# Batch 0 of a packed-attention SwiGLU kernel: one written order, with unsplit fp32 output products

## The chip, the cores and the metric

The kernel runs on one core of a Trainium2 chip. The metric is the device time of one launch in microseconds (us), and lower is better. The times below are medians of several runs; the profile is one execution, recorded by the hardware profiler.

## What is computed

Eight batches of eight heads, 576 positions and 64 features per head go through two attentions. In the first, 32 packed queries `p` attend to `k` and `v`; in the second, `q` attends to the 32 packed rows. The result, 4608 tokens by 512 features, goes through a gated feed-forward layer of width 1536.

```
def sm_attn(qq, kk, vv):
    s = scale * np.matmul(qq, kk.transpose(0, 1, 3, 2))
    s = s - np.max(s, axis=-1, keepdims=True)
    a = np.exp(s)
    a = a / (np.sum(a, axis=-1, keepdims=True) + 1e-09)
    return np.matmul(a, vv)
p_packed = sm_attn(p, k, v)
out = sm_attn(q, p_packed, p_packed)
...
g = x @ w_gate
silu = g * (1.0 / (1.0 + np.exp(-g)))
val = x @ w_val
return (silu * val @ w_out).astype(np.float32)
```

The three weight matrices arrive as 64-bit floats and are converted on the chip.

## The kernel before, in words

**Tiling.** Each batch is 576 tokens. The width 1536 is cut into 12 columns `fc` of 128 (gate and value side by side), and each `fc` is worked in two half chunks: A with 256 tokens and B with 320. Below, "2A" is half chunk A of `fc` 2, and a *quad* is the four half chunks of two neighbouring columns (2A, 2B, 3A, 3B). A half chunk is two sets of six matrix products (L439): the first set gives the gate, the second the value.

**The folded product.** The attention output is never formed. `m_part` multiplies the packed rows (`ppt`) with the gate and value weights `w`, and `gv_chunk` multiplies the result with the attention weights `a2`. Each factor is split into a high part (`mh`, `a2h`) and a low part (`ml`, `a2l`) of a reduced-precision type, and three products of parts stand for one exact one. ScalarE (ACT) makes the high part, VectorE (DVE) the low one. Then ACT computes `sg` (Silu, L446) from the gate set and DVE multiplies it with the value set into `hf` (L451; for B also 64 leftover tokens, L454).

**Output products.** `out_mm` (L459) multiplies `h`, split into `hh` and `hl`, with `w_out`, split into `wo_h` and `wo_l`: three products of 512 columns for each 128 tokens, gathered over the 12 columns in four accumulators `acc`.

**Batch 0** is special, because the weights have to be loaded (`load_w`, `load_wout`) and converted (`convert_w`, `convert_wout`: two passes on ACT, L106 and L107, then three on DVE, L108 to L110). A first loop over the 12 columns computes all half chunks and keeps `h` in `kept`; conversions run two columns ahead. A second loop then does all output products. Batch 1's attention (`aux_of`) is interleaved in both loops. From batch 1 on, output products follow the gate and value products one column behind.

**Buffers.** `gv` has two accumulators, one per set; the gate accumulator is free when Silu has read it, the value accumulator when `hf` (and L454) has. `aux` has two, `sg` one. Loads of weights, `k` and `q` share four `io` buffers, and all are issued by one queue (SyncE, SP), in order.

**Order.** TensorE's (PE) instructions stand in the order in which the program writes them. Those of the other engines are placed by a scheduler, except that from batch 1 on some are pinned to the written order (`pin`).

Of the kernel before, what the change touches and what calls it, by code (L numbers as in the profile page):

```python
# [12 lines left out]
I32 = mybir.dt.int32  # L13
# [13 lines left out]
SC, NSC = 96, 6  # L27
# [14 lines left out]
def tile_pack_attention_swiglu(ctx: ExitStack, tc: tile.TileContext, qT, kT, v, vq, pT, wgv, wout, out):  # L42
# [19 lines left out]

    wide = [True]
# [10 lines left out]
    def ps():  # L74
        turn[0] += 1
        if wide[0] and turn[0] % 2:
            return ps_acc.tile([P, 512], F32, tag="acc", name="acc_aux")
        if wide[0] and turn[0] % 4:
            return ps_gv.tile([P, 512], F32, tag="gv", name="gv_aux")
        return ps_aux.tile([P, 512], F32, tag="aux", name="aux")  # L80
# [19 lines left out]
    def f64_convert(dst, st, shape):  # L100
# [5 lines left out]
        nc.scalar.activation(dst, hi.bitcast(F32), AF.Abs)  # L106
        nc.scalar.activation(lo.bitcast(F32), lo.bitcast(U32), AF.Identity, bias=minus_two, scale=LOW_WORD)  # L107
        nc.vector.tensor_scalar(dst, dst, F64_HI_LEAST, F64_HI_MOST, op0=ALU.max, op1=ALU.min)  # L108
        nc.vector.scalar_tensor_tensor(d, d, 3, lo, op0=ALU.logical_shift_left, op1=ALU.bitwise_or)  # L109
        nc.vector.scalar_tensor_tensor(d, hi, 0x3FFFFFFF, d, op0=ALU.bitwise_or, op1=ALU.bitwise_and)  # L110

    sts, sto, wos = {}, {}, {}
# [4 lines left out]
    def convert_w(fc):  # L117
        f64_convert(w_t[fc // 2][:, :, fc % 2, :], sts.pop(fc), NHP)

    def load_wout(fc):  # L120
        sto[fc] = io_tile([P, 1024, 2], I32, "st")
        nc.sync.dma_start(
            sto[fc].rearrange("p (f n) two -> p f (n two)", f=2), wout[fc : fc + 2].rearrange("f p n -> p f n")
        )

    def convert_wout(fc):
        f = wos[fc] = pool.tile([P, 2, DM], F32, tag="wf", bufs=1, name="wo_f")
        f64_convert(f, sto.pop(fc), 2)

    def slot(dtype, name):  # L130
        return pool.tile([P, DM], dtype, tag="slot", bufs=2 * NFC + 2, name=name)

    wo_h, wo_l = {}, {}
# [9 lines left out]
    def load_k(b):  # L143
        p_t = pool.tile([P, NHP, NP], F32, tag="p", bufs=2, name="p_t")
        (nc.sync if b else nc.scalar).dma_start(p_t, pT[b])
        k_t = io_tile([P, 2, NHP, HS], F32, "k_t")
        for hf in range(2):
# [3 lines left out]
    def load_v(b):  # L151
        if b < NEARLY:
            vs[b] = pool.tile([SC, NSC, H * D], F32, tag="v", bufs=1, name="v_t")
            nc.sync.dma_start(vs[b], v[b])
# [4 lines left out]
    def load_q(b):  # L159
        qs[b] = io_tile([P, 2, NHP, HS], F32, "q_t")  # L160
# [10 lines left out]
    def s1_scores(b, direct):  # L171
# [21 lines left out]
        if direct:  # L193
# [6 lines left out]
            nc.vector.tensor_tensor(rs[:, 0], rs[:, 1], rs[:, 2], op=ALU.add)  # L200

    def s1_exp(b):
        t1, rs, nm = st1[b]
        for par in range(NPAR):
            nc.scalar.activation(
                t1[:, par], t1[:, par], AF.Exp, bias=nm[:, 1, par : par + 1], scale=SCALE, accum_out=rs[:, 0, par : par + 1]
            )

    def s1_post(b):
        t1, rs, _ = st1.pop(b)  # L210
        nc.vector.tensor_scalar(rs[:, 1], rs[:, 0], 1e-9, None, op0=ALU.add)
        nc.vector.reciprocal(rs[:, 2], rs[:, 1])
        a1 = pool.tile([SC, NPAR * NSC, P], F32, tag="a1", bufs=1, name="a1")
        for i in range(0, NPAR * NSC, 4):
            p_t = ps()
            for x in range(4):
                par, c = divmod(i + x, NSC)
                nc.tensor.transpose(p_t[:SC, x * P : (x + 1) * P], t1[:, par, c * SC : (c + 1) * SC], ident)
            copy(
                nc.vector if wide[0] and i == 4 else nc.scalar,  # L220
                a1[:, i : i + 4], p_t[:SC].rearrange("p (c x) -> p c x", x=P),
# [4 lines left out]
        for par in range(NPAR):  # L226
            for c in range(NSC):
# [467 lines left out]
```

## Time and profile before

| | us |
|---|---|
| median of 3 runs | 795.68 (795.36 to 798.3) |
| the profiled execution's own time | 794.16 |
| its span in the profile | 792.4 |
| first gate product of batch 0 | 28.89 |
| first gate product of batch 1 | 150.52 |

In the profile, PE is TensorE's products and PEld its weight loads; DVE is VectorE, ACT ScalarE, POOL GpSimd and SP the queue that issues transfers. A row of the timeline gives start and duration in us, then engine, line, operation, what is written and read, the shape and the count; in brackets stands the idle time ahead of it and what ended that. A row of the groups gives busy time and the mean duration in ns of one instruction. A product in full fp32 appears as two records, one per pass.

### The profile page before, as it was taken

To read this page: it belongs to the slowest core of one execution; us is meant where nothing else is said; L and a number is where in the kernel's file an instruction comes from. 1 tells how busy PE (TensorE), PEld (TensorE's weight loads), DVE (VectorE), ACT (ScalarE), POOL (GpSimd) and SP (SyncE) were. 2 spreads that over 40 slices of the span, in tenths; PEclk is the share of its full clock that TensorE was granted. 3 is DMA by queue.
4 is the path that set the end of the run, shared out by engine and by line. 5 is a ranking of instruction groups with operands and counts; after the bars stand their busy time and mean duration, and the time that the engine had idled before them with its cause. 6 is when DMAs were issued, how large, how long until landed. Compare 5 with 4: busy or idle time off the path is not lost.

```text
span 792.4 us, 14383 instructions
## 1 busy us (share of the span) xinstructions
PE 741.8 (94%) x5866; PEld 598.2 (76%) x5866; DVE 458.4 (58%) x1022; ACT 381.5 (48%) x702; POOL 18.3 (2%) x25
## 2 busy tenths in 40 slices
PE   4469788999999999999999999999999999999998
PEld 2346566778787787878778787777888787888886
DVE  3998786454575545755475554754566454653434
ACT  3679664454452545464272643655362542643331
POOL 0001122000000000000000000000000000000000
PEclk9699999999999999999999999999999999999999
DMA  9866742220301211020301103010101000010001
GB/s 319 303 225 249 257 164 80 94 65 10 119 1 67 67 66 61 27 92 3 101 27 67 65 3 127 1 55 3 67 2 53 15 3 2 1 53 2 1 1 66
DMA packets 19777, 59.10 MB, mean 75 GB/s; under 512 B 5952, under 2 KB 6976, under 8 KB 17216
## 3 DMA queue, kind: packets, MB, share of 16 engines
q1 hardware_dynamic: 19568, 58.12, 21.0%
q8 instruction: 46, 0.75, 0.4%
q14 instruction: 19, 0.16, 0.1%
q10 hardware_dynamic: 144, 0.07, 0.0%
HBM read 48.69 MB, written 9.49 MB: 73 GB/s over the span
## 4 chain that ended last, share of the span: by engine, by line
PE 74%; ACT 13%; DVE 7%; DMA 3%; issue 3%; SPq 0%; DVEq 0%; ACTq 0%
PE gv L439 32%; PE acc L459 29%; PE aux L169 6%; PE aux L459 4%; ACT L446 4%; PE aux L332 2%; ACT sg L446 2%; DMA st<-in_wout 1%; DVE ml L90 1%; ACT mh L84 1%; DVE w L109 1%; ACT hh L84 1%; DMA st<-in_wgv 1%; ACT L375 1%; ACT L280 1%
## 5 line engine op out<-in xcount | busy, mean ns | idle before, releaser
L439 PE MATMUL gv<-a2h,ml 128*128 128x256 f32 (+1 forms) x768 | 175.3, 310 | 24.6 <-ACT sg L446 10.0
L439 PEld LDWEIGHTS gv<-a2h,ml 128*128 128x128 f32 x768 | 128.8, 191 | 60.5 <-ACT sg L446 16.9
L439 PE MATMUL gv<-a2l,mh 128*128 128x256 f32 (+1 forms) x768 | 166.2, 298 | 1.1 <-DVE a2l L397 1.1
L446 ACT ACTIVATE sg<-gv 128x256 f32<-128x256 f32 x192 | 79.2, 412 | 179.7 <-PE gv L439 138.2
L439 PE MATMUL gv<-a2h,mh 128*128 128x256 f32 (+1 forms) x768 | 165.7, 297 | 0.0
L459 PE MATMUL acc<-wo_h,hl 128*128 128x512 f32 x384 | 156.5, 407 | 5.0 <-DVE hl L90 5.0
L451 DVE TENSOR_TENSOR hf<-gv,sg 128x256 f32<-128x256 f32 x168 | 70.7, 421 | 140.0 <-PE gv L439 122.5
L459 PE MATMUL acc<-wo_l,hh 128*128 128x512 f32 x384 | 151.4, 394 | 0.0
L459 PE MATMUL acc<-wo_h,hh 128*128 128x512 f32 x384 | 150.9, 393 | 0.0
L439 PEld LDWEIGHTS gv<-a2l,mh 128*128 128x128 f32 x768 | 125.0, 191 | 1.7 <-DVE a2l L397 1.7
L439 PEld LDWEIGHTS gv<-a2h,mh 128*128 128x128 f32 x768 | 125.3, 192 | 0.0
L84 ACT CAST hh<-hf 128x256 fp32r<-128x256 f32 x168 | 67.8, 404 | 111.7 <-DVE hf L451 111.7
L90 DVE TENSOR_TENSOR hl<-hf,hh 128x256 fp32r<-128x256 f32 x168 | 71.1, 423 | 81.6 <-ACT hh L84 81.1
L459 PEld LDWEIGHTS acc<-wo_h,hl 128*128 128x128 f32 x384 | 72.5, 189 | 51.4 <-issue 35.7
L459 PEld LDWEIGHTS acc<-wo_h,hh 128*128 128x128 f32 x384 | 72.5, 189 | 16.6
L459 PEld LDWEIGHTS acc<-wo_l,hh 128*128 128x128 f32 x384 | 72.7, 189 | 9.6
L90 DVE TENSOR_TENSOR ml<-aux,mh 128x512 fp32r<-128x512 f32 (+1 forms) x106 | 62.4, 628 | 19.3 <-ACT mh L84 19.3
L169 PE MATMUL aux<-w,ppt 64*32 64x512 f32 (+1 forms) x848 | 56.3, 566 | 5.4 <-ACT t L189 5.3
L84 ACT CAST mh<-aux 128x512 fp32r<-128x512 f32 (+1 forms) x106 | 52.1, 544 | 5.6 <-PE aux L169 2.9
L446 ACT ACT_TABLE_LOAD x33 | 42.3, 1283 | 11.3 <-issue 10.6
L107 ACT ACTIVATE st<-st,minus_two 128x1024 f32<-128x1024 uint32 x18 | 22.3, 1242 | 0.0
L169 PEld LDWEIGHTS aux<-w,ppt 64*32 64x32 f32 x848 | 10.4, 106 | 14.6 <-ACT t L189 6.2
(127 smaller groups left out, 616.9 us busy)
## 6 DMA issues: line engine op xcount, KB each, us to landing
st<-in_wgv SPq DMA_DIRECT2D x12, 1024.0 KB, 6.6
k_t<-in_kT SPq DMA_DIRECT2D x16, 576.0 KB, 4.9
q_t<-in_qT SPq DMA_DIRECT2D x16, 576.0 KB, 4.8
out<-ot SPq DMA_DIRECT2D x36, 256.0 KB, 2.1
v_t<-in_vq SPq DMA_DIRECT2D x6, 1280.0 KB, 5.6
st<-in_wout SPq DMA_DIRECT2D x6, 1024.0 KB, 5.6
v_t<-in_v SPq DMA_DIRECT2D x2, 1152.0 KB, 13.4
p_t<-in_pT SPq DMA_DIRECT2D x7, 64.0 KB, 2.9
```

Of the source, the lines that this page charges most:

```text
L84: e.copy(dst, src)
L90: lo.tensor_tensor(dst_l, src, dst_h.bitcast(F32), op=ALU.subtract)
L107: nc.scalar.activation(lo.bitcast(F32), lo.bitcast(U32), AF.Identity, bias=minus_two, scale=LOW_WORD)
L109: nc.vector.scalar_tensor_tensor(d, d, 3, lo, op0=ALU.logical_shift_left, op1=ALU.bitwise_or)
L169: nc.tensor.matmul(outs[par][32 * hp : 32 * hp + 32], lhs(r, hp), rhs(r, hp), start=True, stop=True)
L280: late.append(lambda hs=hs: pin(nc.scalar.activation(e[:, :, hs, :SQ], e[:, :, hs, :SQ], AF.Exp, scale=SCALE)))
L332: nc.tensor.matmul(p_p[D * par : D * par + D, NP * hp : NP * hp + NP], v_t[:, par, hp, k, :], a1[:, par, hp, k, :], start=(k == 0), stop=( ...
L375: pin(nc.scalar.activation(x, x, AF.Exp, scale=SCALE))
L439: nc.tensor.matmul(pg[:, :n], m_[:, g, f, s * P : (s + 1) * P], a_[:, g, off : off + n], start=(i == 0), stop=(i == 5),)
L446: nc.scalar.activation(sg[:, :n], pgs[0][:, :n], AF.Silu)
L451: nc.vector.tensor_tensor(hf, pgs[1][:, o : o + 256], sg[:, o : o + 256], op=ALU.mult)
L459: nc.tensor.matmul(acc[:, :], h_[:, c : c + P], w_[fc], start=(fc == 0 and i == 0), stop=(fc == NFC - 1 and i == 2),)
```

## The change

Batch 0 becomes one loop. Five half chunks behind each half chunk, its output products follow, as single fp32 products of the unsplit `h` and the unsplit `w_out`; nothing in batch 0 is split for them. DVE and ACT, too, follow the written order in batch 0: each half chunk calls `between` after its Silu, which issues a fixed portion of the conversions (now generators, advanced by `steps`). The high and low parts of `w_out` are made during batch 1 and the last products of batch 0 (`split_wout`), the low part on DVE where GpSimd made it before. Further edits: `v` of batches 0 and 1 lies in five chunks of 128 rows (the last one of 64) where it was six of 96; 24 products of `ident` with itself (`warm_up`) are put into the start; the exponentials of the first attention are issued one parity at a time; `m_part` can leave its low parts for `m_lows`.

```diff
-SC, NSC = 96, 6
+NSC = -(-S // P)
...
     def split_wout(fc):
-        f = wos.pop(fc)
-        for i in range(2):
-            wo_h[fc + i], wo_l[fc + i] = slot(F32R, "wo_h"), slot(F32R, "wo_l")
-            split(wo_h[fc + i], wo_l[fc + i], f[:, i], hi=nc.scalar, lo=nc.gpsimd)
+        k, i = divmod(fc, 2)
+        if i == 0:
+            wo_h[k], wo_l[k] = pair(F32R, "wo_h"), pair(F32R, "wo_l")
+        pin(nc.scalar.copy(wo_h[k][:, i], wos[k][:, i]))
+        pin(nc.vector.tensor_tensor(wo_l[k][:, i], wos[k][:, i], wo_h[k][:, i].bitcast(F32), op=ALU.subtract))
...
         nc.scalar.activation(sg[:, :n], pgs[0][:, :n], AF.Silu)
         if late:
             late.pop(0)()
+        between()
...
+            def outs(i):
+                fc, is_b = divmod(i, 2)
                 for c in range(2):
-                    out_mm(accs[2 * i + c], *h, c * P, fc)
+                    nc.tensor.matmul(
+                        accs[2 * is_b + c], half(i)[:, c * P : c * P + P], wos[fc // 2][:, fc % 2],
+                        start=(fc == 0), stop=(fc == NFC - 1),
+                    )
+                    yield
...
+                a, b_, o = 2 * k + 2, 2 * k + 3, ("out", k - 1)
+                more = a < NFC
+                def between():
+                    if slot == 0:
+                        steps(o, 5)
+                        if more:
+                            steps(a, 2)
+                    elif slot == 1 and more:
+                        steps(a, 2)
+                        steps(b_, 2)
+                    elif slot == 2 and more:
+                        steps(a, 1)
+                        steps(b_, 1)
+                    elif slot == 3:
+                        if more:
+                            steps(b_, 2)
+                        steps(("out", k), 2)
+                gv_chunk(0, fc, bool(is_b), nothing, half(i), between)
...
+                for t, _ in enumerate(outs(i - LAG) if i >= LAG else ()):
+                    if t == 0 and slot == 3 and more:
+                        m_part(0, k + 1, both)
+                next(aux, None)
...
+                    if b == 1 and fc > 1 and count[0] in (3, 7):
+                        split_wout(fc - fc % 2 + count[0] // 7) if fc % 2 == 0 else None
```

PE in the middle of batch 0. In the kernel before, around 5B to 6A, gate and value products follow each other, with only small products of `m_part` or of batch 1's attention between them:

```order
L439 MATMUL gv<-a2h,mh 128x320 x2
L246 MATMUL aux<-ident,pp 128x128
L439 MATMUL gv<-a2h,ml 128x256 x2
L439 MATMUL gv<-a2l,mh 128x256 x2
L439 MATMUL gv<-a2h,mh 128x256 x2
L169 MATMUL aux<-w_86,ppt 32x256 x8
L439 MATMUL gv<-a2h,ml 128x256 x2
```

In the changed kernel, at 5B, the end of the quad of columns 4 and 5:

```order
L465 MATMUL gv<-a2h,mh 128x320 x2
L624 MATMUL acc<-wo_f,h_324 128x512
L179 MATMUL aux<-w_84,ppt 32x512 x8
L624 MATMUL acc<-wo_f,h_324 128x512
L179 MATMUL aux<-q_t,ppt 32x288 x8
L465 MATMUL gv<-a2h,ml 128x256 x2
```

Two fp32 output products now stand after every half chunk, and `m_part` comes once a quad for both columns, between them.

DVE in batch 0, before: the scheduler puts a half chunk's multiplication (`h`, L451) between the passes of a conversion (`w_85`, L108 to L110), and takes passes of two conversions in turn:

```order
L451 TENSOR_TENSOR h_311<-gv,sg 128x256
L109 SCALAR_TENSOR_TENSOR w_85<-w_85,st 128x4x256
L108 TENSOR_SCALAR w_85<-w_85 128x4x256
L451 TENSOR_TENSOR h_311<-gv,sg 128x256
L454 TENSOR_TENSOR t_301<-gv,sg 128x64
L110 SCALAR_TENSOR_TENSOR w_85<-st,w_85 128x4x256
L109 SCALAR_TENSOR_TENSOR w_85<-w_85,st 128x4x256
```

DVE in the changed kernel, at the first two half chunks of columns 4 and 5:

```order
L421 TENSOR_TENSOR ml<-aux,mh 128x512 x2
L113 TENSOR_SCALAR wo_f<-wo_f 128x1024
L114 SCALAR_TENSOR_TENSOR wo_f<-wo_f,st 128x1024
L115 SCALAR_TENSOR_TENSOR wo_f<-st,wo_f 128x1024
L478 TENSOR_TENSOR h_325<-gv,sg 128x256
L113 TENSOR_SCALAR w_84<-w_84 128x4x256
L114 SCALAR_TENSOR_TENSOR w_84<-w_84,st 128x4x256
L478 TENSOR_TENSOR h_325<-gv,sg 128x256
L481 TENSOR_TENSOR t_318<-gv,sg 128x64
```

Each multiplication now stands behind the two or three conversion passes of its own half chunk, and passes that depend on each other stand next to each other.

ACT in batch 1, before, over half chunks without attention work:

```order
L446 ACTIVATE sg<-gv 128x320
L84 CAST hh<-hf 128x256
L446 ACTIVATE sg<-gv 128x256
L84 CAST hh<-hf 128x256
L84 CAST mh<-aux 128x512 x2
```

and in the changed kernel:

```order
L472 ACTIVATE sg<-gv 128x320
L89 CAST hh<-hf 128x256
L472 ACTIVATE sg<-gv 128x256
L89 CAST hh<-hf 128x256
L144 CAST wo_h<-wo_f 128x512
L472 ACTIVATE sg<-gv 128x320
```

The high part of one column of `w_out` now stands ahead of a Silu, ten times in batch 1; the low part follows on DVE. From batch 2 on all engines have the order they had.

More of the change, by code (lines that the diff above doesn't have):

```diff
@@ L399, in tile_pack_attention_swiglu, with m_lows, m_part @@
     ms = {}
-    def m_part(b, k, fcs):
+    lows = []
+    def m_lows():
+        while lows:
+            nc.vector.tensor_tensor(*lows.pop(0), op=ALU.subtract)
+    def m_part(b, k, fcs, low=True):
         if (b, k) not in ms:
@@ L485, in aux_of @@
             yield from s1_scores(d, False)
-            if d + 1 < B:
-                load_k(d + 1)
-            s1_exp(d)
+            for par in range(NPAR):
+                late.append(lambda par=par: s1_exp(d, par))
+            yield
             yield
@@ L498, in aux_of @@
             yield
-        if d + 1 < B:
+        if NEARLY <= d < B - 1:
             load_v(d + 1)
@@ L604, in tile_pack_attention_swiglu @@
                 while late:
                     late.pop(0)()
+                run_all(outs(i))
                 next(aux, None)
-            if fc == NFC - 2:
-                for _ in aux:
-                    while late:
-                        late.pop(0)()
-                m_part(1, 0, both)
+                if i == 2 * NFC - 2:
+                    m_part(1, 0, both)
+                    split_wout(0)
+                    split_wout(1)
+            for _ in aux:
+                pass
+            load_q(2)
```

286 lines of the change are left out of this document (176 added, 110 removed).

## The prediction

> **What bounds the kernel now.** I read the page first, then busy time by stage, then PE's timeline and waits.
>
> ```profile
> span 792.4 us, 14383 instructions
> PE 741.8 (94%) x5866; PEld 598.2 (76%) x5866; DVE 458.4 (58%) x1022; ACT 381.5 (48%) x702; POOL 18.3 (2%) x25
> ```
> ```profile
> 30.00:60.00 30.00, 22.54 (x196) 16.49 (x196) 28.91 (x52) 19.32 (x36) 0.00 (x0) 0.90 0.70 233
> 60.00:90.00 30.00, 26.02 (x262) 19.94 (x266) 24.48 (x43) 25.10 (x43) 5.23 (x4) 0.94 0.63 225
> 109.00:150.00 41.00, 36.00 (x174) 27.84 (x159) 26.84 (x49) 18.57 (x37) 7.45 (x6) 0.96 0.29 106
> 150.00:240.00 90.00, 88.70 (x714) 71.69 (x713) 52.20 (x124) 44.69 (x81) 0.20 (x1) 1.00 0.18 61
> ```
> ```profile
> 28.89 0.80 PE L439 MATMUL gv<-a2h,ml 128*128 128x256 f32 x2 [9.62 <-ACT a2h L396]
> ...
> 60.02 1.40 PE L169 MATMUL aux<-w,ppt 64*32 64x256 f32 x16 [3.48 <-ACT t L189]
> ...
> 97.84 0.90 PE L439 MATMUL gv<-a2h,ml 128*128 128x320 f32 x2 [1.43 <-DVE h L451]
> ...
> 121.44 0.79 PE L459 MATMUL acc<-wo_h,hl 128*128 128x512 f32 x1 [5.00 <-DVE hl L90]
> ...
> 150.52 0.40 PE L439 MATMUL gv<-a2h,ml 128*128 128x256 f32 x2
> ```
>
> The columns of the stages are PE, PEld, DVE, ACT and POOL, then granted clock, DMA share and GB/s. From 150 on PE is busy 88.7 of 90 us at clock 1.00: only PE work counts there. Batch 0 is the other regime. PE's first gate product stands at 28.89, batch 1's at 150.52, and in the 121.6 us between them DVE, ACT and PE take turns: from 30 to 60 DVE is full (28.91 of 30) and PE is not. The change can gain here alone, and can lose here and, through the moved splits, in batch 1.
>
> **The products: PE work.** The next rows are PE's timeline; the pace is the distance of starts.
>
> ```profile
> 18.14 0.40 PE L169 MATMUL aux<-q_t,ppt 64*32 64x288 f32 x1
> ...
> 18.38 0.40 PE L169 MATMUL aux<-q_t,ppt 64*32 64x288 f32 x1
> ...
> 104.48 0.72 PE L169 MATMUL aux<-q_t,ppt 64*32 64x288 f32 x16
> 105.13 0.51 PE L439 MATMUL gv<-a2h,ml 128*128 128x256 f32 x2
> ...
> 106.67 0.53 PE L439 MATMUL gv<-a2h,ml 128*128 128x320 f32 x2
> ...
> 108.69 0.71 PE L169 MATMUL aux<-q_t,ppt 64*32 64x288 f32 x16
> ...
> 127.22 0.39 PE L459 MATMUL acc<-wo_h,hl 128*128 128x512 f32 x1
> ...
> 137.87 0.39 PE L459 MATMUL acc<-wo_h,hh 128*128 128x512 f32 x1
> ...
> 146.63 1.09 PE L169 MATMUL aux<-w,ppt 64*32 64x512 f32 x16
> 147.65 0.50 PE L459 MATMUL acc<-wo_h,hl 128*128 128x512 f32 x1
> ```
>
> From 127.22 to 137.87 lie 47 split products, 0.2266 us each, so three cost 0.68. No full-size fp32 product is in this trace. From below: an fp32 pass over 288 columns took 0.24 (18.14 to 18.38), so 512 columns take 0.427, two passes 0.853. From above: `m_part`'s two passes over 512 took 1.02 with both ends. I take 0.89, near the lower end, because consecutive products stream like the lower row. The 48 products then cost 42.7 us against 32.6 for 144 split ones: +10.1 of PE work (+8.3 to +16.4), not below zero in any case. [...]
>
> Half chunk A takes 1.54 (105.13 to 106.67), B 2.02, so a quad 7.1. A quad has eight output products (7.1) and `m_part` (1.02).
>
> **The conversions and the written order.** These are groups by line, with mean ns of one, and two DVE rows of the timeline.
>
> ```profile
> L106 ACT ACTIVATE w<-st 128x1024 f32<-128x1024 f32 x12 | 13.8, 1154 | 7.3 <-DMA st<-in_wgv 7.3
> L107 ACT ACTIVATE st<-st,minus_two 128x1024 f32<-128x1024 uint32 x18 | 22.3, 1242 | 0.0
> L108 DVE TENSOR_SCALAR w<-w 128x1024 f32<-128x1024 f32 x12 | 9.1, 764 | 4.3 <-ACT w L106 4.2
> L109 DVE SCALAR_TENSOR_TENSOR w<-w,st 128x1024 int32<-128x1024 int32 x12 | 14.6, 1220 | 0.9 <-ACT st L107 0.7
> L110 DVE SCALAR_TENSOR_TENSOR w<-st,w 128x1024 int32<-128x1024 int32 x12 | 14.6, 1214 | 0.1
> ...
> L446 ACT ACT_TABLE_LOAD x33 | 42.3, 1283 | 11.3 <-issue 10.6
> L446 ACT ACTIVATE sg<-gv 128x256 f32<-128x256 f32 x96 | 37.1, 387 | 82.9 <-PE gv L439 42.8 <-DVE ot L86 20.4 <-DVE s L355 12.3
> L205 ACT ACTIVATE t<-t,nm 128x576 f32<-128x576 f32 x2 | 1.6, 778 | 0.0
> L375 ACT ACTIVATE s<-s 128x576 f32<-128x576 f32 x16 | 10.9, 684 | 0.1
> L451 DVE TENSOR_TENSOR hf<-gv,sg 128x256 f32<-128x256 f32 x168 | 70.7, 421 | 140.0 <-PE gv L439 122.5 <-ACT sg L446 17.1
> L90 DVE TENSOR_TENSOR ml<-aux,mh 128x512 fp32r<-128x512 f32 x84 | 54.0, 684 | 19.1 <-ACT mh L84 19.1
> L84 ACT CAST mh<-aux 128x512 fp32r<-128x512 f32 x84 | 45.0, 588 | 4.7 <-PE aux L169 2.0
> L370 DVE TENSOR_REDUCE r<-s 128x18 f32<-128x576 f32 x16 | 11.9, 745 | 0.1
> L394 DVE STREAM_TRANSPOSE t<-s 128x576 f32<-128x576 f32 x16 | 12.4, 773 | 0.2
> L84 ACT CAST wo_h<-wo_f 128x512 fp32r<-128x512 f32 x12 | 7.1, 619 | 7.9 <-DVE wo_f L110 4.8 <-DVE hl L90 3.1
> ```
> ```profile
> 84.59 1.21 DVE L109 SCALAR_TENSOR_TENSOR w<-w,st 128x1024 int32<-128x1024 int32 x1
> 85.83 1.23 DVE L110 SCALAR_TENSOR_TENSOR w<-st,w 128x1024 int32<-128x1024 int32 x1
> ```
>
> A conversion is 2.3 us on ACT (1.15 + 1.24, overlapped by 0.1) and 3.2 on DVE. Passes that depend on each other start 1.24 apart, so the written order, which sets them side by side, pays them in full. `hf` stands behind `between`'s passes on DVE; who waits is PE, whose value set needs the accumulator that `hf` frees, and Silu, whose one `sg` buffer `hf` frees.
>
> *Start.* The exponentials now go ahead of the first weight conversion; I put the first transposes of q scores on DVE at 18.0. From there to `hf` of 0A DVE's row is closed: two halves of six 128x576 steps (0.75 each, small ones 0.5: 10.0), four transposes (0.45 estimated: 1.8), two half-size `ml` (0.8) and a conversion (3.2), 15.8 together: 33.8. Then 0A to 1B are a chain. 0B's gate set and the next `m_part` on a cold PE, `mh`, Silu: 3.7. ACT's conversion 2.3, DVE's step 1.2, `hf` and L454 0.6: 4.1. Silu 0.4, ACT's conversion 2.3, two DVE steps 2.4, `hf` 0.6: 5.7. Maxima 0.8, copies 0.4, `m_part` 1.0, `mh` and `ml` 1.8, scores 0.65: 4.6. Column 2 starts at 51.9.
>
> *Quads k = 1 to 4.* ACT has three conversions (6.9), four Silus (1.7), two `mh` (1.2): 9.8. DVE has 9.6, four `hf` and two L454 (2.1), two `ml` (1.4): 13.1. PE has 15.2 (k = 1: 13.4). Batch 1's attention comes on top. k = 1: two exponentials between Silus, four table loads (5.1), 1.6, and two copies (about 1.0), so ACT 17.5. k = 2: the product with `v` (about 1.3) and scores (0.65 by 104.48), PE 17.2. k = 3: four transposes, two maxima with subtraction, one sum (1.8 + 3.0 + 1.2), DVE 19.1. k = 4: four scalings or transposes, a sum, a low part (3.1 + 1.2 + 0.75), DVE 18.2. Together 72.0. Each quad closes with a hand-over, `m_part`, `mh`, `ml`, before the next gate set, in which the bound engine partly waits. Records of independent DVE steps overlap by some 0.08, which gives a little back. Followed operation by operation, the four take 18.7, 18.3, 18.9 and 19.2: 75.1.
>
> *Tail.* Quad 5 is PE work: 7.1, then output products of nine half chunks overall (18 x 0.89 = 16.0), `m_part` 1.0, and 0.9 of waiting for the last `w_out` conversion: 25.0.
>
> Batch 0 ends at 51.9 + 75.1 + 25.0 = 152.0 where it ended at 150.5: **+1.5**. The two serial loops become one, and most of what that saves goes to the dearer products and to dependences.
>
> *Edits taken at nothing.* The 24 `warm_up` products run while PE waits for `p`, for exponentials and (28.89) up to 9.62 us for `a2h`; uncovered they would cost some 5. `v`'s load moves the same bytes. The order of loads changes on SP's queue: weight loads now stand behind batch 1's `v`, which waits for batch 0's product with `v` near 16.
>
> ```profile
> st<-in_wgv SPq DMA_DIRECT2D x12, 1024.0 KB, 6.6
> ```
>
> A load lands 6.6 after its issue, and the buffers free at least 8 ahead of use; only batch 1's `q`, wanted one half chunk (4 us) after its buffer frees, is near, at most 2 us.
>
> *Batch 1.* Ten columns of `w_out` are split: 0.62 on ACT ahead of a Silu, 0.68 on DVE (by `ml`). PE works 1.4 on output products between `hh` and the next gate set, so they fit; I take 0.7, bounds 0 and 6.2.
>
> *Clock.* I add 0.6 for one cold spell on PE's path. The sum is 1.5 + 0.7 + 0.6 = **+2.8**. Against the profiled execution's own 794.16 (span and 1.76 around it) this makes 797.0; the median of the runs lies 1.5 higher, so 798.5.
>
> **The rivals.**
>
> *Faster: the engines overlap better than I followed.* The quads at their sums less the overlaps (70), the start at 48, the tail at 24 give 142, thus 8.5 less than before: 787. For it: the kernel before idles on PE too (22.54 of 30). Against it: `hf` behind the passes. It decides if PE waits less than 1 us a quad.
>
> *Slower: the clock.* Two short waits suffice to halve PE's pace: `m_part` took 1.40 after 3.48 idle, and 97.84 shows a pair at 0.90 (0.53 warm, 106.67) after 1.43. Each quad ends with two waits of 1 to 2 us. A spell of 3.4 at half pace costs 1.7; five of them 8.5: 804 to 807. It decides if the granted clock falls below 0.9 between 50 and 125, and if PE is within 1.7 of the bound there. [...]
>
> *Slower: the splits in batch 1.* If a Silu is late each time, 10 x 0.62 goes onto PE's path: 803. The waits of PE from 150 to 240 (total, times, longest, in us) stand against it:
>
> ```profile
> PE gv L439 <- ACT sg L446: 0.9, 2, 0.6
> ```
>
> PE waited 0.9 for Silu in that whole stage.
>
> **How the numbers follow.** The forecast has 0.45, by itself 793 to 803 (products at 0.853 or 1.02, `q` late or not, each stage's second digit); the first rival 0.25, the clock 0.18, the splits 0.12. A measurement can tell 0.5%, 4.0 us, from no change. Faster by more: the first rival, 0.25. Within: 0.33 of the forecast, 0.04 of the splits, 0.37. Slower: 0.12 of the forecast, 0.18 and 0.08, 0.38. The range is 787 to 807: about 0.1 lies beyond each end.
>
> **What would show it.** Right: fp32 passes 0.43 to 0.46 apart; column 2's first gate set near 52; quads of 18 to 19, the third and fourth with DVE full; batch 1's first gate set near 152 to 153; batch 1 as long as before within 1. Wrong: quads under 17 or over 21, or PE idle for a load, or a batch 1 over 2 longer.

## The result, and the profile after

The changed kernel takes 796.6 us (median of 20 runs, 795.73 to 800.43); the kernel before, run beside it, takes 796.62 (20 runs, 794.36 to 798.37). The ratio is 1.0007, with a 95% interval of 0.9996 to 1.0019: no difference that a measurement can tell. The forecast was 798.5, within 787 to 807. The profiled execution of the changed kernel took 796.16 us, against 794.16 before: +2.0 where the sum said +2.8.

Two lines of the page of the changed kernel, and its group of the fp32 output products (busy time and mean ns of one record, then the idle time ahead):

```profile
span 794.4 us, 14060 instructions
PE 750.8 (95%) x5750; PEld 590.0 (74%) x5750; DVE 457.5 (58%) x1002; ACT 376.2 (47%) x670; POOL 2.0 (0%) x13
...
L624 PE MATMUL acc<-wo_f,h 128*128 128x512 f32 x96 | 45.9, 598 | 0.9 <-DVE wo_f L115 0.9
```

PE is 9.0 us busier, and the span is only 2.0 longer. The stages of the changed kernel (PE, PEld, DVE, ACT, POOL, granted clock, DMA share, GB/s), first the start, then cut at the first gate set of each quad, of the tail and of batch 1, show where that went:

```profile
30.00:52.00 22.00, 13.59 (x106) 9.48 (x107) 13.83 (x24) 12.67 (x19) 0.00 (x0) 0.77 0.40 143
51.20:69.69 18.49, 14.69 (x91) 9.56 (x85) 12.50 (x21) 17.67 (x24) 0.00 (x0) 1.00 0.68 232
69.69:88.32 18.63, 18.23 (x183) 11.20 (x181) 12.71 (x21) 10.46 (x15) 0.00 (x0) 1.00 0.63 233
88.32:106.61 18.29, 15.63 (x104) 9.51 (x97) 15.72 (x25) 14.44 (x17) 0.00 (x0) 1.00 0.62 226
106.61:125.85 19.24, 15.82 (x81) 9.53 (x81) 17.45 (x29) 11.55 (x15) 0.20 (x1) 1.00 0.46 151
125.85:150.57 24.72, 23.60 (x101) 13.20 (x101) 10.71 (x17) 5.77 (x10) 0.00 (x0) 1.00 0.43 152
```

In the first quad ACT is the fullest engine (17.67 of 18.49), in the second PE (18.23 of 18.63), in the fourth DVE (17.45 of 19.24), in the tail PE (23.60 of 24.72). In the third no engine is full: DVE and PE are level (15.72 and 15.63 of 18.29). The clock is 1.00 from 51.20 on, and 0.77 in the start.

PE's timeline gives the first gate set of each quad, and the waits at two hand-overs:

```profile
51.20 0.50 PE L465 MATMUL gv<-a2h,ml 128*128 128x256 f32 x2
...
69.28 0.66 PE L226 MATMUL aux<-ident,t 128*128 128x128 f32 x4 [2.71 <-DVE ml L421]
69.69 0.57 PE L465 MATMUL gv<-a2h,ml 128*128 128x256 f32 x2
...
88.32 0.50 PE L465 MATMUL gv<-a2h,ml 128*128 128x256 f32 x2
...
106.61 0.38 PE L465 MATMUL gv<-a2h,ml 128*128 128x256 f32 x1 [1.18 <-DVE ml L421]
...
123.31 1.09 PE L179 MATMUL aux<-w,ppt 64*32 64x512 f32 x16 [1.84 <-DVE w L115]
...
125.85 0.38 PE L465 MATMUL gv<-a2h,ml 128*128 128x256 f32 x1 [0.39 <-DVE ml L421]
...
142.68 5.42 PE L624 MATMUL acc<-wo_f,h 128*128 128x512 f32 x12 [0.91 <-DVE wo_f L115]
148.03 1.09 PE L179 MATMUL aux<-w,ppt 64*32 64x512 f32 x16
...
150.57 0.58 PE L465 MATMUL gv<-a2h,ml 128*128 128x256 f32 x1
```

Batch 0 ends at 150.57 where it ended at 150.52. From 142.68 to 148.03 lie 12 fp32 records, 0.446 us each: a product costs 0.89, as taken.

Batch 1 is where the profile lost its 2 us. The next batch's first gate set stands at 248.84 (246.87 before), so batch 1 takes 98.27 instead of 96.35; after it, both kernels take the same. PE's waits from 150 to 249, then ACT's rows and PE's row at one of the two:

```profile
PE gv L465 <- ACT sg L472: 2.7, 2, 1.6
```
```profile
168.10 0.69 ACT L297 ACTIVATE e<-e 128x576 f32<-128x576 f32 x1
...
168.98 0.61 ACT L144 CAST wo_h<-wo_f 128x512 fp32r<-128x512 f32 x1
169.61 1.28 ACT L472 ACT_TABLE_LOAD   x1
170.91 0.44 ACT L472 ACTIVATE sg<-gv 128x320 f32<-128x320 f32 x1
```
```profile
171.40 0.50 PE L465 MATMUL gv<-a2h,ml 128*128 128x256 f32 x2 [1.11 <-ACT sg L472]
```

The split's cast stands between an exponential and the table load for the next Silu, and PE waits for that Silu. The other wait, 1.59 at 224.72, ends in the same way: from the cast at 217.35 to the Silu at 224.23 ACT's row is closed. Together they are 2.7 us where the kernel before waited 0.9.

### The profile page after: what moved, and what is told of

It is laid out like the page before. It is cut to its first block, busy times and chain, and to the rows that moved or that the text cites. A ratio compares the mean times of both kernels' runs of the same rounds, so it can differ in the third digit from the quotient of the medians.

```text
span 794.4 us, 14060 instructions
## 1 busy us (share of the span) xinstructions
PE 750.8 (95%) x5750; PEld 590.0 (74%) x5750; DVE 457.5 (58%) x1002; ACT 376.2 (47%) x670; POOL 2.0 (0%) x13
## 3 DMA queue, kind: packets, MB, share of 16 engines
q1 hardware_dynamic: 19792, 58.12, 20.5%
## 4 chain that ended last, share of the span: by engine, by line
PE 71%; ACT 10%; DVE 3%; issue 2%; ACTq 0%; DVEq 0%
PE gv L465 31%; PE acc L486 25%; PE aux L179 6%; PE aux L486 4%; ACT L472 4%; PE aux L349 2%; PE acc L624 2%; ACT sg L472 1%; DVE ml L421 1%; ACT mh L438 1%; ACT L297 1%; ACT hh L89 1%; ACT L392 1%; PE aux L284 1%; ACT s L392 1%
## 5 line engine op out<-in xcount | busy, mean ns | idle before, releaser
L465 PE MATMUL gv<-a2h,ml 128*128 128x256 f32 (+1 forms) x768 | 178.0, 313 | 24.3 <-ACT sg L472 13.7
L486 PE MATMUL acc<-wo_h,hl 128*128 128x512 f32 x336 | 136.6, 406 | 0.0
L486 PE MATMUL acc<-wo_l,hh 128*128 128x512 f32 x336 | 132.2, 393 | 0.0
L486 PE MATMUL acc<-wo_h,hh 128*128 128x512 f32 x336 | 131.6, 392 | 0.0
L486 PEld LDWEIGHTS acc<-wo_h,hl 128*128 128x128 f32 x336 | 63.2, 188 | 42.5 <-issue 34.4
L486 PEld LDWEIGHTS acc<-wo_h,hh 128*128 128x128 f32 x336 | 63.1, 188 | 14.5
L486 PEld LDWEIGHTS acc<-wo_l,hh 128*128 128x128 f32 x336 | 63.3, 188 | 7.7
L179 PE MATMUL aux<-w,ppt 64*32 64x512 f32 (+1 forms) x768 | 52.7, 602 | 5.0 <-DVE w L115 3.3
L624 PE MATMUL acc<-wo_f,h 128*128 128x512 f32 x96 | 45.9, 598 | 0.9 <-DVE wo_f L115 0.9
L624 PEld LDWEIGHTS acc<-wo_f,h 128*128 128x128 f32 x96 | 16.6, 189 | 17.0 <-issue 15.2
```

The source lines that it names most:

```text
L179: nc.tensor.matmul(outs[par][32 * hp : 32 * hp + 32], lhs(r, hp), rhs(r, hp), start=True, stop=True)
L465: nc.tensor.matmul(pg[:, :n], m_[:, g, f, s * P : (s + 1) * P], a_[:, g, off : off + n], start=(i == 0), stop=(i == 5),)
L486: nc.tensor.matmul(acc[:, :], h_[:, c : c + P], w_[fc // 2][:, fc % 2], start=(fc == 0 and i == 0), stop=(fc == NFC - 1 and i == 2),)
L624: nc.tensor.matmul(accs[2 * is_b + c], half(i)[:, c * P : c * P + P], wos[fc // 2][:, fc % 2], start=(fc == 0), stop=(fc == NFC - 1),)
```

## Experiments

Theory 1, limits in turn, is that of the prediction: ACT, PE and DVE bound batch 0 in turn, and an edit counts only in the stage that its engine bounds. Theory 2: the dearer products count throughout. Theory 3: the written order of `hf` behind the conversion passes holds the loop. Theory 4, formed after the first runs: the clock, which falls after PE's idle time, is part of the price. In the table, the median is followed by its ratio to the kernel before with the 95% interval; then, from each profiled execution, the start of column 2, the four quads, the tail and batch 1, in us.

| run | median | ratio to before | column 2 | 1 | 2 | 3 | 4 | tail | batch 1 |
|---|---|---|---|---|---|---|---|---|---|
| changed kernel | 796.60 | 1.0007 (0.9996 to 1.0019) | 51.20 | 18.49 | 18.63 | 18.29 | 19.24 | 24.72 | 98.27 |
| half | 793.66 | 0.9958 (0.9942 to 0.9973) | 51.44 | 18.73 | 17.06 | 18.26 | 20.10 | 22.97 | 98.26 |
| halffill | 788.86 | 0.9900 (0.9885 to 0.9916) | 49.98 | 18.55 | 16.70 | 18.28 | 19.24 | 20.44 | 98.28 |
| more | 808.93 | 1.0146 (1.0123 to 1.0168) | 52.54 | 19.29 | 21.64 | 20.21 | 19.24 | 31.20 | 97.84 |
| hfirst | 814.22 | 1.0221 (1.0208 to 1.0235) | 53.40 | 22.74 | 22.23 | 19.88 | 25.15 | 25.32 | 98.31 |
| oneexp | 794.83 | 0.9982 (0.9973 to 0.9991) | 50.75 | 16.91 | 18.61 | 18.29 | 19.24 | 24.70 | 98.28 |
| splitpool | 798.44 | 1.0023 (1.0007 to 1.0039) | 51.69 | 19.03 | 19.50 | 18.28 | 19.53 | 27.33 | 96.50 |
| splitdve | 797.04 | 1.0002 (0.9988 to 1.0015) | 52.18 | 19.13 | 21.03 | 18.29 | 19.24 | 24.70 | 97.48 |
| nowarm | 798.47 | 1.0023 (1.0008 to 1.0037) | 52.37 | 18.80 | 19.75 | 18.30 | 19.24 | 24.70 | 98.29 |
| fill | 795.28 | 0.9986 (0.9976 to 0.9997) | 50.16 | 18.53 | 18.62 | 18.28 | 19.24 | 24.71 | 98.26 |
| best3 | 794.53 | 0.9976 (0.9964 to 0.9989) | 52.34 | 17.69 | 18.63 | 18.28 | 19.23 | 25.24 | 97.48 |
| best4 | 792.53 | 0.9947 (0.9935 to 0.9959) | 50.13 | 16.91 | 18.62 | 18.29 | 19.25 | 24.69 | 97.51 |

**Half the columns** (half).

```diff
-                        accs[2 * is_b + c], half(i)[:, c * P : c * P + P], wos[fc // 2][:, fc % 2],
+                        accs[2 * is_b + c][:, : DM // 2], half(i)[:, c * P : c * P + P], wos[fc // 2][:, fc % 2, : DM // 2],
```

> Batch 0's output products cover 256 of 512 columns (the other half of batch 0's outputs is left out and filled with copies of the first half), so 48 fp32 products lose about 0.445 us each, 21.4 us of PE work. Theory 1 (batch 0's length is set in turn by ACT in the first quad, PE in the second and the tail, DVE in the third and fourth): only the stages that PE bounds shorten, the tail by 6 to 8 and the second quad by 2 to 3, the third and fourth by less than 1 each; together -9 (-7 to -11), ratio to the changed kernel 0.987 to 0.991. Theory 2 (the dearer products hold throughout): -21, ratio 0.973. Theory 3 (the written order of hf behind the conversion passes holds the loop): the quads stay and only the tail moves, -6 to -7.

Of 21.4 us of PE work, the median lost 2.9 against the changed kernel. Theory 2 falls, but 2.9 is also a third of what theory 1 said. The place was right for the second quad (-1.6) and the tail (-1.75), not the size; the fourth quad even grew by 0.9. The fourth quad, the tail and the whole from 52 to 150 show why:

```profile
105.49:125.59 20.10, 16.03 (x80) 11.62 (x80) 17.45 (x29) 11.52 (x15) 0.20 (x1) 0.75 0.50 167
125.59:148.56 22.97, 19.96 (x100) 16.27 (x101) 10.79 (x18) 5.82 (x11) 0.00 (x0) 0.81 0.40 143
52.00:150.00 98.00, 77.86 (x545) 60.20 (x544) 70.03 (x112) 59.95 (x83) 0.20 (x1) 0.88 0.56 198
```

The granted clock, 1.00 in the changed kernel, is 0.88 here. PE had less to do, idled more (busy for 77.86 of the 98 us, against 86.60), and was then slowed: two records of 256 columns took 0.64 together at 126.57, and 0.40 at 88.66 in the changed kernel.

**The same with the idle gaps filled** (halffill). Products of no use stand where PE waits: identity products into an accumulator that is not yet in use, and products with zeros later.

```diff
+            def early_keep(n):
+                for _ in range(n):
+                    nc.tensor.matmul(accs[3][:, :P], ident, ident, start=True, stop=True)
+            def keep(n):
+                for _ in range(n):
+                    nc.tensor.matmul(accs[0][:, :P], zero, ident, start=False, stop=False)
...
             gv_chunk(0, 0, False, nothing, half(0), first_a)
+            early_keep(22)
...
                     if t == 0 and slot == 3 and more:
+                        keep(KEEP[k][0])
                         m_part(0, k + 1, both)
+                if slot == 3 and more:
+                    keep(KEEP[k][1])
```

> The kernel with half the columns in batch 0's output products (the other half left out and filled with copies), plus the fillers in the start and at its larger hand-over gaps, 9 of them ahead of the last w_out column. Without fillers it gained 3 us of 21.4 us of PE work, at a granted clock of 0.88 from 52 to 150. Theory 4 (the clock took much of the rest): the clock goes to 0.97 or more, the fourth quad from 20.1 to 18.5 or less and the tail from 23.0 to 20.5 or less, time 3 to 6 us below the run with half the columns. Theory 1 (DVE and ACT bound the quads, the last w_out conversion the tail): within 1 us of it, whatever the clock.

```profile
68.53:85.23 16.70, 16.70 (x198) 13.30 (x196) 12.52 (x21) 10.32 (x15) 0.00 (x0) 1.00 0.68 246
103.51:122.75 19.24, 15.55 (x104) 12.38 (x104) 17.45 (x29) 11.62 (x15) 0.21 (x1) 1.00 0.45 153
122.75:143.19 20.44, 18.44 (x119) 15.37 (x118) 10.78 (x18) 5.82 (x11) 0.00 (x0) 1.00 0.48 173
```

These are the second quad, the fourth and the tail. Doing more work on PE, the kernel became 4.8 us faster than half, and all its four runs lie between 788.68 and 788.91. The clock is 1.00 in every quad and the tail. The tail is 20.44 (expected 20.5 or less), the fourth quad 19.24 (expected 18.5 or less). So theory 4 holds, and theory 1 can be read with the clock held, against fill below: halving the products takes 1.9 from the second quad, 4.3 from the tail, and nothing (0.0 each) from the first, third and fourth. On the medians that is 6.4, in the stages that theory 1 named, but under its 7 to 11. Part of the rest is the fillers: halffill has 106 of them, fill 74, and eight of the difference stand in the second quad, where PE has no gap (16.70 of 16.70). At 0.25 us each (54 of them keep PE busy for 13.5) they are 2.0, about what that quad lacks (1.9 gained of 3.6 shed). The tail gives 4.3 of the 8.0 that its 18 products shed: PE's waits for `h` from 25 to 155 are 5.1 us, against 1.3 in fill.

**Half the columns once more** (more).

```diff
+                    nc.tensor.matmul(
+                        accs[2 * is_b + c][:, : DM // 2], half(i)[:, c * P : c * P + P], wos[fc // 2][:, fc % 2, : DM // 2],
+                        start=False, stop=(fc == NFC - 1),
+                    )
```

> Each of batch 0's 48 fp32 output products is followed by one more over 256 of the 512 columns (so these columns of batch 0's outputs are doubled): 48 x 0.446 = 21.4 us of PE work more, the mirror image of the run with half the columns, without idle time that could let the clock fall. Theory 1 (limits in turn; PE has 2.9 to 3.8 us of idle time in the first, third and fourth quad, almost none in the second and the tail): of 3.6 us more in each quad, the first, third and fourth lengthen by 0 to 1.5, the second by 2.5 to 3.6, the tail by 7 to 8; together +12 (+10 to +14), ratio 1.013 to 1.018 to the changed kernel. Theory 2 (PE work counts throughout): +21, ratio 1.027.

The median rose by 12.3: theory 1's +12. The second quad took +3.0, the tail +6.5 (7 to 8 expected), the first +0.8 at a clock of 0.89, the fourth nothing, and the third +1.9, more than the 1.5 expected at most. The profile's start, too, is 1.3 longer (the granted clock of the whole execution is 0.985, against 0.991), which the expectation had left out, so that the sum came out so near is partly luck. The third and fourth quad:

```profile
93.47:113.68 20.21, 19.00 (x120) 12.55 (x113) 15.81 (x25) 14.39 (x17) 0.00 (x0) 1.00 0.59 210
113.68:132.92 19.24, 18.47 (x97) 12.54 (x97) 17.46 (x29) 11.76 (x15) 0.20 (x1) 1.00 0.41 134
```

In the third quad PE had 2.7 us without work, and the 3.6 added made it the fullest engine. In the fourth PE went from 15.82 to 18.47 us, and the quad stayed at 19.24, as it did with less PE work in halffill: its length does not hang on PE.

**`hf` ahead of the passes** (hfirst).

```diff
-        between()
         hf = pool.tile([P, 256], F32, tag="hf", bufs=2, name="hf") if kept is None else kept
...
+        between()
         return h_split(hf, nc.scalar, nc.vector) if kept is None else None
```

> hf (and L454) stand ahead of between's conversion passes on DVE and ACT. Theory 3 (the written order of hf holds the loop): the waits of gate and value products for DVE's t and h (3.1 and 1.5 us in batch 0) go, -3 to -5 us. Theory 1 (limits in turn): where DVE or ACT is full, putting hf first only moves the wait to what stands behind the passes, so -1.5 to +1.5 us, with the waits of m_part for w and ml growing by what the others lose.

Both were wrong: 17.6 us slower than the changed kernel. PE's waits from 25 to 155, then DVE at the fourth quad (its gate set at 118.25; in the changed kernel at 106.61), here and in the changed kernel:

```profile
PE aux L179 <- DVE w L115: 14.8, 4, 5.2
```
```profile
122.06 0.42 DVE L477 TENSOR_TENSOR h<-gv,sg 128x256 f32<-128x256 f32 x1 [2.10 <-ACT sg L472]
122.41 0.68 DVE L113 TENSOR_SCALAR wo_f<-wo_f 128x1024 f32<-128x1024 f32 x1
```
```profile
108.24 0.63 DVE L113 TENSOR_SCALAR wo_f<-wo_f 128x1024 f32<-128x1024 f32 x1
```

In the changed kernel the passes start 1.6 us after the gate set and run while PE makes the value set. With `hf` first, DVE stands idle for 2.10 us, until that set and its Silu are done, and the passes start 4.2 us after the gate set. PE's waits for a converted `w` at the hand-overs grow from 3.3 in two places to 14.8 in four. The clock was 0.80 to 0.92 in the four quads, so part of the 17.6 is the clock's, which this run doesn't separate. Theory 3 falls: the written order that the prediction counted as a burden here hides the passes.

**Both exponentials in one step** (oneexp).

```diff
-            for par in range(NPAR):
-                late.append(lambda par=par: s1_exp(d, par))
+            late.append(lambda: [s1_exp(d, par) for par in range(NPAR)])
```

> Both exponentials of batch 1's first attention are issued behind one Silu instead of two, which saves two table loads (2.56 us of ACT) in the first quad. Theory 1 (ACT bounds the first quad): the quad from 32... to be exact the 18.5 us from column 2's first gate set to column 4's fall by 1.5 to 2.6 and batch 0 ends as much earlier. Theories 2 and 3 (PE work, or DVE's written order): the quad stays within 0.5, because ACT is not what ends last there.

The quad fell from 18.49 to 16.91, the other stages stayed; the median lost 1.8. ACT is what ends last there, as theory 1 said. The hand-over that waited 2.71 in the changed kernel (its row at 69.28) now reads:

```profile
67.25 0.66 PE L226 MATMUL aux<-ident,t 128*128 128x128 f32 x4 [0.40 <-DVE ml L421]
```

**The splits on GpSimd** (splitpool).

```diff
-        pin(nc.scalar.copy(wo_h[k][:, i], wos[k][:, i]))
-        pin(nc.vector.tensor_tensor(wo_l[k][:, i], wos[k][:, i], wo_h[k][:, i].bitcast(F32), op=ALU.subtract))
+        pin(nc.gpsimd.tensor_copy(wo_h[k][:, i], wos[k][:, i]))
+        pin(nc.gpsimd.tensor_tensor(wo_l[k][:, i], wos[k][:, i], wo_h[k][:, i].bitcast(F32), op=ALU.subtract))
```

> Both halves of the w_out split, the high part (a cast) and the low part (a subtraction), run on GpSimd instead of ACT and DVE. If the splits are what made batch 1 1.9 us longer (ACT's cast pushes a Silu by up to 1.6 us next to the exponentials): batch 1's length goes from 98.3 back to 96.4 and the time falls by 1.5 to 2 us. If the batch's +1.9 in the two profiles has another cause (the copies' place, the tail of batch 0): batch 1 stays at 98.3 and the time within 0.5. Above 0 only if GpSimd's slower passes make a product wait for wo_l: +1 to +5.

Batch 1 went from 98.27 to 96.50 (96.35 before the change): the splits are what lengthened it. Yet the median rose by 1.8, by a way that none of the expectations had. GpSimd began while `w_out` was still being converted, and here are two of DVE's passes beside it, the `hf` wait behind them on PE, and the same two passes in the changed kernel:

```profile
129.47 1.77 DVE L113 TENSOR_SCALAR wo_f<-wo_f 128x1024 f32<-128x1024 f32 x1
...
132.82 2.17 DVE L115 SCALAR_TENSOR_TENSOR wo_f<-st,wo_f 128x1024 int32<-128x1024 int32 x1
```
```profile
135.38 0.56 PE L465 MATMUL gv<-a2h,ml 128*128 128x320 f32 x2 [2.57 <-DVE h L478]
```
```profile
126.97 0.69 DVE L113 TENSOR_SCALAR wo_f<-wo_f 128x1024 f32<-128x1024 f32 x1
...
128.96 1.23 DVE L115 SCALAR_TENSOR_TENSOR wo_f<-st,wo_f 128x1024 int32<-128x1024 int32 x1
```

Beside GpSimd 0.69 became 1.77 and 1.23 became 2.17, while `hf`, with one input in an accumulator, stayed at 0.41 to 0.42. What they contend for, the run doesn't show. In the profile the tail is 2.6 longer for it. The first two quads, which the edit doesn't reach, are 1.4 longer at clocks of 0.88 and 0.94.

**The cast on DVE in batch 1** (splitdve).

```diff
+        if steady[0]:
+            pin(nc.vector.tensor_copy(wo_h[k][:, i], wos[k][:, i]))
+        else:
+            pin(nc.scalar.copy(wo_h[k][:, i], wos[k][:, i]))
```

> In batch 1 the cast of w_out's high part moves from ACT to DVE, ahead of the subtraction that stands there already. If ACT's cast next to a table load is what made batch 1 longer: batch 1 falls from 98.3 to about 96.5 and the time by 1.5 to 2 us (0.998), without the price that GpSimd's passes had. Rival (10 more passes of 0.6 us on DVE push hf and low parts instead): batch 1 stays between 97.5 and 99, time within 0.7.

Batch 1 fell to 97.48, by 0.8: the near end of the rival's range, not the 96.5. The median is 0.4 above the changed kernel's, as the rival said (within 0.7). This profiled execution is the slowest of twelve (795.0 to 799.07) and its second quad took 21.03 at a clock of 0.87, in code that this edit does not touch, so the two medians don't resolve a gain of 0.8.

**The unsplit products in the old loops** (b_unsplit; in batch 0 the low part of `w_out` is left out).

```diff
-                h = h_split(kept[fc][:, 256 * i : 256 * i + 256], nc.scalar, nc.vector)
...
-                    out_mm(accs[2 * i + c], *h, c * P, fc)
+                    nc.tensor.matmul(
+                        accs[2 * i + c], kept[fc][:, 256 * i + c * P : 256 * i + c * P + P], wo_h[fc].bitcast(F32),
```

> The kernel before, with its two loops, but with fp32 output products of the unsplit h (w_out's high part stands in for w_out, so its low part is left out of batch 0's outputs). This prices the dearer products alone. By the prediction's terms: 48 x 0.89 - 144 x 0.2266 = +10.1 us of PE work in the second loop, less the 5.0 us for which that loop waited for the first low part of h: batch 1's first gate product goes from 150.5 to about 155.6, time +5 (+3 to +7), ratio 1.004 to 1.009. Rival (the second loop waits for the conversions of w_out anyway): 0 to +2. Rival (nothing of it is given back): +10.

The median is 796.39, ratio 1.0003 (0.9990 to 1.0015): +0.1, not +5. Its profiled execution, the slowest of twelve, took 798.13, 4.0 over that of the kernel before, with batch 1's first gate set 3.75 later. The start of the second loop in the kernel before, then PE's rows here:

```profile
109.34 0.50 PE L459 MATMUL acc<-wo_h,hl 128*128 128x512 f32 x1
```
```profile
112.15 38.03 PE L602 MATMUL acc<-wo_h,h 128*128 128x512 f32 x88
150.11 1.09 PE L169 MATMUL aux<-w,ppt 64*32 64x512 f32 x16
...
154.27 0.80 PE L439 MATMUL gv<-a2h,ml 128*128 128x256 f32 x2
```

88 records from 112.15 to 150.11, 0.431 each, without a gap: a product costs 0.863 in an unbroken run, nearer to the lower bound of 0.853 than to the 0.89 taken. The 48 then cost 41.4 us, 8.8 more than 144 split ones. But 2.8 of the 3.75 stand ahead of the second loop (112.15 against 109.34), where the edited products don't reach; 1.5 of them are there at the first gate set of batch 0 already (30.37 against 28.89). The loop itself went from 41.2 us (109.34 to 150.52) to 42.1: +0.9, near the +0.1 of the medians. The 5.0 that PE waited for the first low part is gone, and with it a cold spell, at a clock of 0.50 from 121.39 to 124.80: in the kernel before, the eight steps from 121.44 to 124.92 took 3.48 us, where eight at 0.2266 take 1.81. The expectation left this spell out. Its first rival (0 to +2) has the size, by another way: PE never waits in this loop.

**Without the warm-up products** (nowarm: the loop in `warm_up` runs over `range(0)`).

> The 24 warm_up products of the start are left out; they change no result. The prediction took them at nothing because PE waits there. If they only fill idle time and keep the clock up: 0 to +2 us, with a lower granted clock from 8 to 24. If they delay the products behind them: -0.5 to -2 us.

The median rose by 1.9. Passes over 288 columns in the start, here and in the changed kernel:

```profile
16.27 0.69 PE L179 MATMUL gv_aux<-q_t,ppt 64*32 64x288 f32 x1 [0.36 <-ACT ppt L265]
...
16.75 0.68 PE L179 MATMUL gv_aux<-q_t,ppt 64*32 64x288 f32 x1
```
```profile
15.62 0.43 PE L179 MATMUL gv_aux<-q_t,ppt 64*32 64x288 f32 x1 [0.36 <-ACT ppt L265]
...
15.88 0.40 PE L179 MATMUL gv_aux<-q_t,ppt 64*32 64x288 f32 x1
```

They start 0.48 apart instead of 0.26: without the warm-up products PE makes these passes at about half pace, as expected. (The profile's clock figure from 8 to 24, 0.96, doesn't show this. In the kernel before, the clock is first recorded where it rises, at 15.57, and the figure counts the time ahead as full, though passes of this size start 0.48 apart there, at 6.40 and 6.88, and 0.24 apart at 18.14 and 18.38.) The first gate set of 0A comes at 24.44 instead of 23.29, column 2 begins 1.2 later, and the second quad took 1.1 more, at a clock of 0.92. The products cost nothing, as taken, and they pay.

**Filled gaps in the changed kernel** (fill; the edit of halffill with 74 fillers instead of 106. The 62 of the expectation is a miscount, and a filler takes 0.23 us, 22 of them 5.07 us, not 0.125).

> 62 filler products (identity or zeros, 128 columns, 0.125 us a pair of records) stand in the places where PE waited in the changed kernel's batch 0: 10 more ahead of 0A, 42 between 0A and column 2, 22 at the hand-overs of the first, third and fourth quad. They change no result. Theory 4 (a cold clock after PE's idle gaps is part of the time, and differs from run to run): the granted clock from 30 to 52 rises from 0.77 to 0.95 or more, no stage after 52 falls below 0.98, the start shortens by 1 to 2 us, and the median falls by 1 to 2.5 us (0.997 to 0.999 to the changed kernel). Rival (the chain of conversions and hand-overs on DVE and ACT sets these stages, PE's pace does not): within 0.7 us, whatever the clock.

```profile
30.00:52.00 22.00, 18.31 (x156) 13.46 (x154) 14.71 (x24) 13.70 (x22) 0.00 (x0) 0.92 0.46 147
```

The median fell by 1.3 and the start by 1.04. The runs, which spread from 795.73 to 800.43 in the changed kernel, now lie between 794.86 and 796.07. The clock of the start rose to 0.92, short of the 0.95 expected.

**Edits together** (best3, with the gate and value products of 0A moved ahead of the second half's normalisation; best4, with 68 of the fillers in its place).

> Three edits to the changed kernel together: one step for both exponentials of batch 1's first attention (measured -2.0 in the profile), the cast of w_out in batch 1 on DVE (-1.8 by the previous entry), and the gate and value products and the Silu of half chunk 0A ahead of the second half's normalisation in the start (0 to -2: it takes PE's 5.99 us wait for 0A's Silu from the chain). Theory 1 lets them add, since each lies in a stage that its engine bounds: -4.5 (-3 to -6), ratio 0.993 to 0.997 to the changed kernel. Rival (a stage's next engine takes over, or the start's work only moves behind 0A's hf): -2 or less.

> Three edits to the changed kernel together: one step for both exponentials of batch 1's first attention (measured -1.8 us on the median), w_out's high part cast on DVE in batch 1 (batch 1 1.8 us shorter in the profile, 0.4 longer on the median at a lower clock), and the fillers against the cold clock in the start and at the hand-overs. If the three add: -4 us (-3 to -5.5), median 791.5 to 794. Rival (the fillers and the cast give nothing on the median): -1.8, 794.8.

best3 gave 2.1 us, less than the sum; in its profiled execution, the slowest of twelve, the start was late at 52.34, at a clock of 0.58 from 30 to 52, and no gain of moving 0A shows. best4 is 4.1 us below the changed kernel, at 792.53 (792.32 to 793.15), and faster than both kernels. Its expectation misquotes the cast's gain in batch 1: the profile of splitdve shows 0.8, not 1.8. The parts add: 1.8 for the exponentials and 1.3 for the fillers on the medians, and 0.8 for the cast in the profile's batch 1 (97.51 here), are 3.9.

## Why the prediction was right, point by point

- **The bound.** Only batch 0, and batch 1 through the splits, moved. From batch 2's first gate set to the end the kernel before took 545.5 us (792.4 - 246.87), and the changed kernel the same (794.4 - 248.84).
- **The products.** 0.89 taken, 0.89 in the tail, 0.863 in the unbroken run. What the prediction made of them is not borne out: most of what the one loop saves was to go to the dearer products, but in the two old loops these cost +0.1 on the median (b_unsplit), because a wait (5.0) and a cold spell (1.7 longer than at full pace) go with them. The rest of the change, from the one loop to the splits in batch 1, brought nothing on the median either (796.39 to 796.60).
- **Start.** `hf` of 0A was put at 33.8 and stood at 32.55; column 2 at 51.9, and at 51.20. The chain between them was 0.55 longer than followed, at a clock of 0.77.
- **Quads and tail.** 18.7, 18.3, 18.9, 19.2 and 25.0 forecast; 18.5, 18.6, 18.3, 19.2 and 24.7 measured. That ACT bounds the first is shown by oneexp, that PE bounds the second and most of the tail, and not the fourth, by more and halffill. That DVE bounds the fourth rests on its busy time and on PE's waits for it (1.84 at 123.31): no run took work off DVE there. The third was to be DVE's, and is shared (15.72 and 15.63 of 18.29). Batch 0 ended 1.4 earlier than forecast, half of it in the start, and its end at 150.57 missed the 152 to 153 given as a sign.
- **Batch 1: a term that was mis-sized.** 0.7 taken, 1.92 measured. The step set the cast's 0.62 against PE's 1.4 us of output products, and left out that it queues on ACT behind an exponential and ahead of a table load of 1.28. splitpool, which takes the splits off ACT and DVE, gave 1.77 of it back. The rival that priced all ten at 0.62 was too dear: PE waited twice. The sign "as long as before within 1" was missed. That batch 0 came out 1.4 below its term and batch 1 1.2 above is luck: the two nearly cancel in the sum.
- **Clock.** 0.6 taken, without a working, where the rival prices one spell at 1.7; filling the gaps gave 1.3. This is what the clock costs the changed kernel, not the difference to the kernel before, whose own cold spells no run fills. In the profiled execution the quads were never cold (1.00), so the rival didn't occur there. That it can occur, half and halffill show (0.88 and 1.00 from 52 to 150), and the runs of the changed kernel agree: those at a mean clock of 0.991 took 795.7 to 796.2, those at 0.978 took 800.1 and 800.4. The rival's spell of 3.4 had no row beside it; the trace before has three of 3.41 at a clock of 0.50, from 59.95, 97.49 and 121.39 on. The step that failed is the reading of the row at 97.84 (a cold pair after 1.43 us idle) as a rule on the length of a wait. In the changed kernel a wait of 2.71 left the clock at 1.00; the last section has what the traces show of the clock.
- **From the profile to the median.** The prediction put the median 1.5 above the profiled execution. Over 20 runs it lies 2.5 above for the kernel before and 0.4 for the changed one; the profiles' +2.0 therefore became 0.0. Of the 1.9 by which 798.5 was too high, the sum brings 0.8, and this step the rest. It carried over the distance of one execution to a median of three, and nothing in the record bears out a fixed distance.
- **Edits taken at nothing.** nowarm prices the warm-up products. The chunks of `v` and the order of the loads have no run of their own; from 25 to 155 PE waits for no load.
- **The faster rival.** Its condition, less than 1 us of waiting a quad, was not met: PE waited 2.71 at 69.28 alone. The order of `hf`, held against it, is not what prevented it: hfirst is slower.

## What to carry to other kernels

Price an edit in each stage by the engine that is full there: 21 us of PE work less or more moved this kernel by 6 (at a held clock) or 12, and a step of 2.6 us on ACT by nearly 2. Where TensorE waits often, cheap products in the gaps can be worth more than saved work (4.8 against 2.9 us in the runs with half the columns), and they narrow the spread of the runs (794.86 to 796.07 in fill, 795.73 to 800.43 without). On an engine that follows the written order, work that is ready belongs ahead of work that waits for another engine (hfirst, the other way round, was 17.6 us slower, part of it by the clock). Before a saved wait is counted, look whether a cold spell goes with it (in the second loop of the kernel before, 3.48 us for eight steps worth 1.81).

## What the runs showed of the hardware

**The clock changes on a grid.** In steps of 0.5 us, half shows the granted clock (third number from the right) fall in these rows:

```profile
69.50:70.00 0.50, 0.50 (x3) 0.50 (x4) 0.50 (x2) 0.00 (x0) 0.00 (x0) 0.58 0.00 0
103.50:104.00 0.50, 0.46 (x2) 0.00 (x1) 0.00 (x0) 0.50 (x1) 0.00 (x0) 0.72 0.44 82
120.50:121.00 0.50, 0.00 (x0) 0.00 (x0) 0.47 (x2) 0.50 (x2) 0.00 (x0) 0.78 1.06 433
141.00:141.50 0.50, 0.00 (x0) 0.00 (x0) 0.50 (x1) 0.00 (x0) 0.00 (x0) 0.76 0.00 0
```

The clock is at 1.00 ahead of each and at 0.50 behind it, so the means place the falls at 69.58, 103.72, 120.78 and 141.26. Their distances are 34.14, 17.06 and 20.48: 10, 5 and 6 times 3.41. Every rise and fall up to 155 in half, the changed kernel and the kernel before lies on such a grid, each execution with its own phase: the falls of the changed kernel are at 23.19, 30.02 and 40.26, those of the kernel before at 22.40, 59.95, 97.49 and 121.39. PE's busy time (first column) in stretches of that grid, the first two ahead of a fall, the third not:

```profile
100.31:103.72 3.41, 1.54 (x18) 0.48 (x18) 2.25 (x4) 3.40 (x4) 0.00 (x0) 1.00 0.48 165
117.37:120.78 3.41, 1.58 (x8) 1.18 (x8) 3.38 (x5) 0.99 (x3) 0.20 (x1) 1.00 0.67 211
...
96.90:100.31 3.41, 2.28 (x13) 1.61 (x12) 3.38 (x6) 2.28 (x4) 0.00 (x0) 1.00 0.57 199
```

Of the 14 falls in the three traces, 13 followed a stretch in which PE was busy for 46% or less, and one a stretch of 60%; one stretch just under 50% caused none. A wait need not fill a stretch: this one, in half, lies for 1.87 us in the stretch ahead of the fall at 103.72:

```profile
102.18 1.09 PE L179 MATMUL aux<-w,ppt 64*32 64x512 f32 x16 [2.27 <-DVE w L115]
```

The longer wait of 2.71 at 69.28 in the changed kernel is shared by two stretches (the border is at 67.56), in which PE was busy for 71 and 50%, and the clock stayed. Busy time alone is no sharp limit. In the traces of these three kernels and of fill, up to 155 us, each of the 14 full-speed stretches with PE busy for 46% or less was followed by a fall, one of the 13 between 49 and 63%, and none of the more than 100 above. The phase differs from run to run; whether the spread of the runs comes from that, no run shows.

**GpSimd beside VectorE** stretched a conversion pass from 0.69 to 1.77 us and another from 1.23 to 2.17, in splitpool.
